# Keeping attention output channel-major from the value product to the output product, with the gate on GpSimd

## The chip, the cores and the metric

The kernel is a single program on one core of a Trainium2 chip. The metric is the device time of one execution in microseconds (us); of several runs the median is taken. The engines that matter are TensorE (PE, with its weight loads as PEld), VectorE (DVE), ScalarE (ACT), GpSimd (POOL) and SyncE (SP), which here only issues DMAs.

## The reference, cut to what matters

One transformer block over 2048 rows of 512 channels in float32: adaptive layer norm, attention of 32 heads of 16 channels, computed in 4 segments of 512 rows, with a compressive memory between segments, then a feed-forward layer with 1792 hidden units. The attention part is:

```
for s in range(4):                       # segments of 512 rows
    logits = einsum("bhqd,bhkd->bhqk", qs, ks) * scale + mask
    p = softmax(logits, axis=-1)
    a_dot = einsum("bhqk,bhkd->bhqd", p, vs)
    pq = phi(qs)                         # phi(t) = t + 1 if t > 0 else exp(t)
    num = einsum("bhld,bhde->bhle", pq, M)
    den = einsum("bhld,bhd->bhl", pq, z)[..., None] + 1e-6
    a_mem = num / den
    o = g * a_mem + (1.0 - g) * a_dot    # g = sigmoid(beta), one number per head
    M = M + einsum("bhld,bhle->bhde", pk, vs)
    z = z + einsum("bhld->bhd", pk)
x = x + ga * (concat(o) @ wo)            # then a second layer norm and
x = x + gb * (relu(h @ w1 + b1)**2 @ w2 + b2)
```

In segment 0 the memory is empty, so `o` there is only `(1 - g) * a_dot`.

## The kernel before

**Units.** Attention is worked in 16 units `u = 4*s + cc`: segment `s` and a group `cc` of 128 channels, which are 8 heads. A unit has two quads (`qd` 0 and 1) of 4 heads. The dense products are done in two float32r parts (high and low) with three matmuls for each product: high·high, high·low, low·high.

**What a unit runs.** `qk` makes q and k with the channels on partitions (`bqk`, L734); ACT and DVE copy them to `sg`, and SP's DMAs put each head's 16 rows at its place in `ST`. `a_quad` computes scores (`ba`, L847) only to find each row's maximum, which DVE takes (L852); the maxima are turned on PE (`bat`, L917), copied by ACT to `mt`, and written by DMA into a spare row of `ST`. `b_quad` computes the scores again with the maximum subtracted by that row (`bpb`, L1017), ACT takes the exponential (L1034), POOL cuts the causal triangle (L1021), and `bpv` (L1076) multiplies by the values. Its result has channels on partitions: one bank of 128 partitions by 512 rows for a quad, 32 partitions per head, of which the first 16 are the head's output channels and the 17th is the softmax denominator. ACT copies the bank to `oraw` (L1100).

**The way back to rows.** After both quads, `turn_o` (L1107) transposes the unit's output by 16 small matmuls (`bfin`, L1111) in two phases, between which a one-element POOL memset (`hinge`, L493) keeps apart two row tiles that swap banks. The normalisation (`norms`: reciprocal L1138, product with 1-g L1140, product L1141) is then done by DVE with rows on partitions, into `on`.

**The memory.** `mem` reads the memory with 16 small matmuls per unit of segments 1 to 3 (`bmr`, L944), also with rows on partitions, and DVE gates it (`den` L951, reciprocal, `am` L954). POOL adds `am` to `on` (L1147), SP stores `on` to `o_dram` in DRAM (L1150). In the last segment the add is on DVE, and the result stays on the chip in `X1L`. The rest of `mem` (`pkt`, `bmu`) updates the memory block `MB`.

**The output product.** `wo_tile(g)` takes 128 rows: it loads `ot` from `o_dram` (L1198) and the block's input rows `xw` (L1199), turns `ot` by 4 transposes (`bwot`, L1209), splits it into high (ACT, L1215) and low (DVE, L1217) parts `oT`, does 12 matmuls (`bwop`, L1182 to L1184), adds the input (DVE, L1224) and takes the statistics of the second layer norm. `blnq` (L599) are that norm's transposes, after which DVE and ACT apply scale and shift (`ln_affine`, L605 and L607) and split the result into the feed-forward's input `H2a` (L612). The feed-forward is `bh` (L1342 to L1344) and `bpf` (L1370 to L1372), with weights loaded through two buffers `wr` (L1308, L1316).

**The order.** The program is a list of nodes with an engine, a cost, a due time, predecessors, and buffers taken from pools of fixed size. The order on each engine is not the planner's choice: the table `ORDER` holds the node numbers of every engine in sequence, and the engine's next node is always the next number. `pe("R")`, `pe("C")` and `pe("F")` mark work that uses the PE array as 64-row tiles, as 32-column tiles, or whole. The first feed-forward node waits for all the nodes of attention:

```
N_FFN = op("NIL", 0.0, open_ffn, -20.0, after=list(PL.nodes))
```

Of the kernel before, what the change touches and what calls it, by code (L numbers as in the profile page):

```python
# [18 lines left out]
P = 128  # L19
# [39 lines left out]
8 47 28 68 41 32 70 49 56 17 35 3 23 66 27 83 58 85 92 16 40 75 65 87 89 14 22 94 15 19 10 96 98 106 112 59 43 63 42  # L59
124 29 55 62 25 45 67 60 73 50 61 118 74 34 24 9 46 48 172 162-163 173 164 174 77 175 51 36 165 31 52 166 69 167 37  # L60
168 64 176 20 53 169 177-178 30 72 26 179 11 39 13 57 12 18 76 21 38 71 44 54 33 327-330 198 332 199 333-334 200-201
232 335 242 203-205 240 206 484-485 251 486-487 245 270 489-490 237 491 215-218 492 261 220-221 247 222 356 264 223
259 747 742 273 608-609 256 275 610 427 282 611 290 285 613 278 614 364 615 266 616 366 375 369 294 383 752 295-296
430 298 385 361 305 308 757 551 371 313 380 301 554 513 388 398 317 518 432 390 318-319 532 761 321 439 762 323 435
763 447 764 521 526 406 451 442 766 455 767 675 523 768-769 458 542 414 452-453 537 528 400 408 416 462 470 866 637
422 928 540 465 929-930 645 545 474-476 424 556 931 650 563 933-934 642 935 547 559 936 794-795 656 647 796-797 478
566 799-800 480 571 801-802 661 575 652 579 576 582 999 586 678 577 589 669 828 598 594 666 1061 664 680 599-600 687
671 1062 836 1063 690 602 1064 847 604 683 1066-1067 695 841 1068 869 1069 838 833 1342 699-701 703 811 855 812 710
# [141 lines left out]
2369 2368 2371-2372 2276 2375 2379 2570 2377-2378 2540 2376 2295 2580 2550 2398 2590 2560 2417 2600 2638 2746 2645  # L210
2637 2736 2636 2766 2673 2756 2641 2652 2659 2680 2648 2666 2687 2676 2694 2655 2776 2662 2701 2669 2697 2729 2715
2683 2708 2690 2722 2704 2718 2711 2732 2725 3569 3153 3156 3364 3358 3563 2948 3361 2951 3566 3159 3367 2954 3572
2957 3162
""",
}

# [1205 lines left out]
```

## Time and profile before

| | before |
|---|---|
| median of 3 runs | 811.79 us (811.22 to 814.17) |
| profiled execution, its own time | 813.31 us |
| its span, first to last instruction | 811.6 us |
| mean granted PE clock | 0.975 |
| PE busy | 790.8 us, 97% of the span, 6177 instructions |
| PE weight loads busy | 617.7 us, 76% |
| DVE busy | 539.8 us, 67% |
| ACT busy | 441.8 us, 54% |
| POOL busy | 222.3 us, 27% |
| DMA traffic | 65.35 MB, mean 81 GB/s |

How to read it: the span is what the profiler saw from the first instruction to the last; the execution's own time has 1.7 us around it. Busy shares are over the whole span, and the span has stages of two kinds: attention until about 472 us, and the feed-forward after it. The profile's rows that the prediction uses are shown there.

### The profile page before, as it was taken

Reading aid. Unit: us, or ns where it says so; the run is one execution under the profiler, and the core shown is the slowest. Engines: PE = TensorE matmul, PEld = TensorE weight load, DVE = VectorE, ACT = ScalarE, POOL = GpSimd, SP = SyncE. Lnnn points to the kernel's source line nnn. Section 1 sums busy time; section 2 is a strip of 40 time slices with the busy share of each in tenths; the row PEclk is TensorE's granted clock in tenths of the full one; section 3 lists DMA queues with packets and bytes.
Section 4 is the critical chain, followed back from the end, with each engine's and each line's share of the span. In section 5 each row is a group of like instructions: output and inputs, shape, how many; then the busy total and the mean of one; then the engine's idle time right before and its main releaser. Section 6 shows DMA issues by size and latency. Waiting matters only on the chain.

```text
span 811.6 us, 16841 instructions
## 1 busy us (share of the span) xinstructions
PE 790.8 (97%) x6177; PEld 617.7 (76%) x6177; DVE 539.8 (67%) x1514; ACT 441.8 (54%) x950; POOL 222.3 (27%) x334
## 2 busy tenths in 40 slices
PE   9999999999998999999999989999999999999997
PEld 8988667686776757876667658888887888888886
DVE  5478859888778797879988877786545343223223
ACT  1457976879876798588855744544223323222221
POOL 3263464347555476354522210000000000000000
PEclk7899989999999999999999999999999999999999
DMA  9454572234133251334532133321100010001001
GB/s 319 123 137 126 163 200 80 71 92 96 52 93 93 63 127 54 99 76 109 154 101 80 53 117 95 101 78 53 40 13 1 1 39 14 1 1 52 1 1 52
DMA packets 51308, 65.35 MB, mean 81 GB/s; under 512 B 7829, under 2 KB 24985, under 8 KB 51226
## 3 DMA queue, kind: packets, MB, share of 16 engines
q1 hardware_dynamic: 51074, 64.14, 28.2%
q8 instruction: 49, 0.80, 0.4%
q14 instruction: 33, 0.27, 0.1%
q10 hardware_dynamic: 152, 0.13, 0.0%
HBM read 29.91 MB, written 7.34 MB: 46 GB/s over the span
## 4 chain that ended last, share of the span: by engine, by line
PE 55%; DVE 5%; ACT 1%; issue 1%; POOL 0%; DVEq 0%; ACTq 0%
PE bh L1342 6%; PE bh L1343 6%; PE bh L1344 6%; PE bpf L1370 6%; PE bpf L1371 6%; PE bpf L1372 6%; PE bqk L734 3%; PE bpv L1076 3%; PE bpb L1017 2%; PE ba L847 2%; PE bwop L1182 2%; DVE ba L852 1%; PE bv L814 1%; PE bwop L1183 1%; PE bwop L1184 1%; PE bwot L1209 1%
## 5 line engine op out<-in xcount | busy, mean ns | idle before, releaser
L852 DVE CUSTOM_DVE_ANT_0 ba<-ba,msk 128x512 f32<-128x512 f32 (+2 forms) x384 | 185.9, 542 | 44.8 <-PE ba L847 39.2
L1034 ACT ACTIVATE pt<-bpb 128x512 f32<-128x512 f32 x320 | 173.3, 609 | 27.0 <-PE bpb L1017 25.3
L1359 DVE TENSOR_TENSOR r<-r 128x512 f32<-128x512 f32 x56 | 38.7, 691 | 128.1 <-ACT rr L1356 128.1
L1021 POOL TENSOR_SCALAR_AFFINE_SELECT pt<-pt 128x512 f32<-128x512 f32 x128 | 80.1, 644 | 89.6 <-ACT pt L1034 71.2
L734 PE MATMUL bqk<-HT,WQK 64*128 64x512 f32 x720 | 104.2, 398 | 0.0
L1352 ACT ACTIVATE r<-bh,b1c 128x512 f32<-128x512 f32 x56 | 38.5, 688 | 108.4 <-DVE rr L1360 55.8
L1370 PE MATMUL bpf<-W,rr 128*128 128x512 f32 x224 | 88.2, 394 | 0.0
L1371 PE MATMUL bpf<-W,rr 128*128 128x512 f32 x224 | 87.6, 391 | 0.0
L1372 PE MATMUL bpf<-W,rr 128*128 128x512 f32 x224 | 87.5, 391 | 0.0
L1017 PE MATMUL bpb<-ST 64*128 64x256 f32 (+2 forms) x512 | 82.8, 361 | 2.4 <-DVE oT L1217 0.5
L1076 PE MATMUL bpv<-pt,VT 128*32 128x512 f32 (+3 forms) x1024 | 81.8, 445 | 0.6 <-POOL pt L1021 0.3
L847 PE MATMUL ba<-ST 63*128 63x256 f32 (+2 forms) x512 | 78.1, 347 | 2.5 <-DVE mx L852 2.1
L734 PEld LDWEIGHTS bqk<-HT,WQK 64*128 64x128 f32 x720 | 74.2, 186 | 6.4 <-ACT ac L885 1.7
L1017 PEld LDWEIGHTS bpb<-ST 64*128 64x128 f32 x512 | 52.9, 188 | 24.8 <-DVE mx L852 5.9
L847 PEld LDWEIGHTS ba<-ST 63*128 63x128 f32 x512 | 54.8, 189 | 20.9 <-DVE mx L852 4.7
L1356 ACT ACTIVATE rr<-r 128x512 fp32r<-128x512 f32 x56 | 35.4, 632 | 55.9 <-PE bpf L1372 55.2
L605 ACT ACTIVATE lnf<-blnq,modc 128x128 f32<-128x128 f32 x88 | 34.2, 470 | 43.0 <-PE blnq L599 40.8
L1076 PEld LDWEIGHTS bpv<-pt,VT 128*32 128x32 f32 x1024 | 27.6, 111 | 36.0 <-issue 27.5
L814 PE MATMUL bv<-WVO,HT 64*128 64x512 f32 x384 | 54.2, 395 | 0.8 <-ACT phi L780 0.8
L852 DVE DVE_READ_ACCUMULATOR2_ANT mx<- 128x1 f32 x384 | 53.7, 140 | 0.0
L1372 PEld LDWEIGHTS bpf<-W,rr 128*128 128x128 f32 x224 | 42.1, 188 | 9.1
L1370 PEld LDWEIGHTS bpf<-W,rr 128*128 128x128 f32 x224 | 42.1, 188 | 9.1
(164 smaller groups left out, 1528.8 us busy)
## 6 DMA issues: line engine op xcount, KB each, us to landing
ST<-sg SPq DMA_DIRECT2D x192, 128.0 KB
wr<-in_B_w SPq DMA_DIRECT2D x28, 256.0 KB
xt<-in_A_x SPq DMA_DIRECT2D x16, 256.0 KB
wm<-in_w_mod SPq DMA_DIRECT2D x16, 256.0 KB
xw<-in_A_x SPq DMA_DIRECT2D x16, 256.0 KB
o_dram<-on SPq DMA_DIRECT2D x12, 256.0 KB
ot<-o_dram SPq DMA_DIRECT2D x12, 256.0 KB
out<-X SPq DMA_DIRECT2D x12, 256.0 KB
```

The source lines that it names most:

```text
L734: m = nc.tensor.matmul(bank(("qk", u, w)), W3(w, k, x, cc * P, (cc + 1) * P)[z], HT[z, y, k], start=(ph == 0 and k == 0 and i == 0), stop= ...
L814: m = nc.tensor.matmul(bank(("v", s, t)), HT[z, x, k, t * P:(t + 1) * P], WVO[z, k, y], start=(ph == 0 and k == 0 and i == 0), stop=(ph == ...
L847: nc.tensor.matmul(dst[:, c0:c0 + n], ST[b:b + 63, 0, sl, qt * P:(qt + 1) * P], ST[b:b + 63, 1, sl, :n], start=True, stop=True)
L852: nc.vector.tensor_tensor_reduce(i, i, msk[:, 512 - n:], scale=1.0, scalar=-3e38, op0=ALU.add, op1=ALU.max, accum_out=o)
L1017: nc.tensor.matmul(dst, ST[b:b + 64, 1, sl, kb * P:(kb + 1) * P], ST[b:b + 64, 0, sl, q0:512], start=True, stop=True)
L1021: nc.gpsimd.affine_select(out=ap, in_=ap, pattern=[[0, ap.shape[1]], [1, P]], compare_op=ALU.is_ge, fill=0.0, base=0, channel_multiplier=-1)
L1034: ns = [act(512, lambda j=j: nc.scalar.activation(buf("PPP"[n], pt)[:, i + j], bank(keys[j]), AF.Exp, scale=0.25), pr[slot] + 0.01 + 0.001 ...
L1076: nc.tensor.matmul(bank(o)[32 * hq:32 * hq + 32, q0:q0 + src.shape[1]], v[:, a:a + 32], src, start=start, stop=stop, tile_position=(0, 32 ...
L1342: nc.tensor.matmul(p, wh, h2[:, 0, k], start=(k == 0), stop=False)
L1370: nc.tensor.matmul(p, rh, FF["W2"][:, f, 0], start=(f == 0), stop=False)
L1371: nc.tensor.matmul(p, rh, FF["W2"][:, f, 1], start=False, stop=False)
L1372: nc.tensor.matmul(p, rl, FF["W2"][:, f, 0], start=False, stop=(f == NF - 1))
```

## The change

The output of the value product is not turned back to rows. It goes to DRAM as it is and comes back with the unit's 128 channels packed on 128 partitions; it is gated there, and the output product takes its stationary operand from it directly.

- `turn_o`, its hinge and `norms` go, and so do the 4 transposes `bwot` of every `wo_tile`, the pools `am` and `on`, and `o_dram`.
- The memory is read with channels on partitions too: two matmuls of 68x512 (`bmr`, now L950) in the place of 16 of 128x68; ACT copies both to `ar` (L954) and SP stores `ar` to `o_raw` (L956). `ar` shares the pool of two buffers with `oraw`, which now holds both quads.
- A new function `heads_out` follows each unit: SP stores `oraw` to `o_raw` (L1119, 512 KB), loads the denominators `den` (L1132, L1134) as 128 partitions of 32 numbers, and the packed values into slots 0 and 2 of `X1L` (L1137, L1140). DVE makes the factors g/den and (1-g)/den on 128x2x32 numbers (L1145 to L1149), SP stores them to `o_gate` (L1153) and loads each back, repeated for the 16 channels of a head, into slots 1 and 3 of `X1L` (L1156). POOL does two products and one sum of 128x512 (L1159; in segment 0 one product), and SP stores the result to `o_turned` (L1174). The 4 slots of `X1L` are one set, used by one unit after another.
- `wo_tile` loads `ot` from `o_turned` with channels on partitions (L1220); ACT makes the high part (L1235), and the low part is on POOL (L1237), in the last segment on DVE. `xw` is a load of its own (L1224).
- The last segment's gating nodes (`LATE`) are no longer ahead of `N_FFN`, so the feed-forward's first nodes may stand before them.
- The gate's numbers `ge` and `omg` are one per partition and group (4 small loads in place of one), a pool `lnf` of two buffers takes over a use of `oraw`, and the `ORDER` tables of all engines are new. The planner's constants are the same.

```diff
-            def read():
-                for t in range(4):
-                    for r in (0, 1):
-                        z = slice(64 * r, 64 * r + 64)
-                        nc.tensor.matmul(bank(bs[r])[:, t * 4 * VA:(t + 1) * 4 * VA], TL[q_][z, t * P:(t + 1) * P],
-                                         MB[z, cc, r * 4 * VA:(r + 1) * 4 * VA], start=True, stop=True)
+            def read():
+                for r in (0, 1):
+                    z = slice(64 * r, 64 * r + 64)
+                    nc.tensor.matmul(bank(bs[r])[:4 * VA, :], MB[z, cc, r * 4 * VA:(r + 1) * 4 * VA], TL[q_][z, :], start=True, stop=True)
...
+            n = [act(512, lambda r=r: nc.scalar.copy(buf("oraw", ar)[:4 * VA, r], bank(bs[r])[:4 * VA, :]), pr[0] + 0.01, after=[n], put=[bs[r]])
+                 for r in (0, 1)]
+            AMN[u] = sp(lambda: nc.sync.dma_start(o_raw[u][2 * P:].rearrange("(r p) n -> p r n", r=2), TL[ar][:4 * VA]), pr[0] + 0.02, 1 << 18,
+                        after=n, put=[ar])
...
+    def heads_out(u, pr):
...
+        def load_d():
+            nc.sync.dma_start(den()[:, 0], rows(0, 2 * P, 32)[:, DH].rearrange("h (i j) -> h i j", j=32))
+            if s:
+                nc.sync.dma_start(den()[:, 1], rows(2 * P, VROW, VA)[:, DH].rearrange("h (i j) -> h i j", j=32))
...
+        def store_g():
+            m = 2 if s else 1
+            nc.sync.dma_start(o_gate[u][0:m].rearrange("o h (i j) -> (h i) o j", j=32), den()[:, 0:m])
+        def load_g(i):
+            nc.sync.dma_start(X1L[:, 1 + 2 * i], o_gate[u][i][:, None, :].to_broadcast([NB, DH, 512]))
+        def times(k, f, op_):
+            return lambda: nc.gpsimd.tensor_tensor(X1L[:, k], X1L[:, k], X1L[:, f], op=op_)
...
+        if s:
+            lg.append(in_turn(3, sp(lambda: load_g(1), pr + 0.06, 1 << 18, after=[w], **own(3))))
+            m.append(op("POOL", 1.24, times(2, 3, ALU.mult), pr + 0.07, after=[lg[1], l[2]], **done(3)))
+            m.append(op("POOL", 1.24, times(0, 2, ALU.add), pr + 0.08, after=m, **done(2)))
+        OUT[u] = sp(lambda: nc.sync.dma_start(o_turned[s][cc * P:(cc + 1) * P, :], X1L[:, 0]), pr + 0.09, 1 << 18, after=[m[-1]], **done(0))
+        if s == NS - 1:
+            LATE.extend(l + [g, w] + lg + m + [OUT[u]])
...
-        n = pe("F", 0.387, tr, pr, after=heads + [N_FFN] if last else [ld], get=[("#D", b), (pool, ot)], put=() if last else [o])
...
-        l = dve(512, lambda: nc.vector.tensor_tensor(TL[ot][:, 1], bank(b), TL[ot][:, 0].bitcast(F32), op=ALU.subtract), pr + 0.01,
-                after=[h], put=[b])
+        l = op("DVE" if last else "POOL", 0.6 if last else 1.24, lambda: (nc.vector if last else nc.gpsimd).tensor_tensor(
+            TL[ot][:, 1], TL[o], TL[ot][:, 0].bitcast(F32), op=ALU.subtract), pr + 0.01, after=[h], put=[o])
...
-    N_FFN = op("NIL", 0.0, open_ffn, -20.0, after=list(PL.nodes))
+    N_FFN = op("NIL", 0.0, open_ffn, -20.0, after=[n for n in PL.nodes if n not in LATE])
```

Three places of the new order. First SP's queue between two units, before, in segment 2: `on` is an attention output going to DRAM, `mt` and `sg` are the rows for `ST`.

```order
L925 DMA ST<-mt 1x8x128 x2
L1150 DMA o_dram<-on 128x4x128
L925 DMA ST<-mt 1x8x128 x2
L789 DMA ST<-sg 32x2x512 x12
L925 DMA ST<-mt 1x8x128 x2
```

The same queue after, around the gating of unit 9 (segment 2): `o_raw_74` is the packed output, `o_raw_75` the memory's part of the same unit, `o_gate_90` the factors.

```order
L1140 DMA X1L<-o_raw_74 128x1x512
L1119 DMA o_raw_74<-oraw 128x2x512
L935 DMA ST<-mt 1x8x128 x2
L1132 DMA den<-o_raw_74 128x1x32
L1137 DMA X1L<-o_raw_74 128x1x512
L1134 DMA den<-o_raw_75 128x1x32
L1153 DMA o_gate_90<-den 128x2x32
L1156 DMA X1L<-o_gate_90 128x1x512 x2
L935 DMA ST<-mt 1x8x128 x2
```

Where one store stood between the rows for `ST`, there are now seven issues that wait on one another, with `mt` rows between and behind them.

Second, POOL in the same segment, before: `pt` are the triangles of the exponentials, `ac` of the row maxima.

```order
L1021 AFFINE_SELECT pt<-pt 128x4x128 x4
L1147 TENSOR_TENSOR on<-on,am 128x512
L893 AFFINE_SELECT ac<-ac 128x4x128
L493 MEMSET hinge_s 1x1
L1021 AFFINE_SELECT pt<-pt 128x4x128
```

POOL after, at unit 9's gating (`hinge_s` here is a hinge of the value projection `bv`, which PE waits for):

```order
L1018 AFFINE_SELECT pt<-pt 128x4x128
L903 AFFINE_SELECT ac<-ac 128x4x128
L1159 TENSOR_TENSOR X1L<-X1L 128x512
L497 MEMSET hinge_s 1x1
L1159 TENSOR_TENSOR X1L<-X1L 128x512 x2
L1018 AFFINE_SELECT pt<-pt 128x4x128 x4
```

A hinge and four triangles now stand behind products that wait for the loads of `o_gate`.

Third, PE at the end of attention, before: the last value products, then the way to the first feed-forward products.

```order
L1076 MATMUL bpv<-pt,VT_113 32x256 x4
L599 MATMUL blnq<-ident,xh 128x128 x4
L1111 MATMUL bfin<-ident,oraw 128x64 x16
L1209 MATMUL bwot<-ident,X1L 128x128 x12
L1182 MATMUL bwop<-WVO,oT 128x512
```

PE after, behind the last value products:

```order
L1073 MATMUL bpv<-pt,VT_148 32x512 x4
L1073 MATMUL bpv<-pt,VT_148 32x384 x4
L1073 MATMUL bpv<-pt,VT_148 32x128 x4
L1073 MATMUL bpv<-pt,VT_148 32x256 x4
L1205 MATMUL bwop<-WVO,oT 128x512
```

and, 47 further `bwop` and 8 further `blnq` later, the first feed-forward products:

```order
L1207 MATMUL bwop<-WVO,oT 128x512
L609 MATMUL blnq<-ident,xh 128x128 x8
L1362 MATMUL bh<-H2a,W_7341 128x512
L1363 MATMUL bh<-H2a,W_7341 128x512
L1364 MATMUL bh<-H2a,W_7341 128x512
```

Four output tiles (48 `bwop`) and all 16 norm transposes of the feed-forward's first input now stand between the last value products and the first `bh`; before, most of them stood ahead of the last value products.

DVE at the same place, before: the last normalisation, the low parts of two output tiles, and the low parts of the first three weight tiles `W_7749`, which `bh` multiplies with.

```order
L1141 TENSOR_TENSOR X1L<-bfin,dn 128x4x64
L1138 RECIPROCAL dn<-bfin 128x16
L1140 TENSOR_TENSOR dn<-dn,omg 128x16
L1141 TENSOR_TENSOR X1L<-bfin,dn 128x4x64
L1147 TENSOR_TENSOR X1L<-X1L,am 128x4x128
L1217 TENSOR_TENSOR oT<-bwot,oT 128x512 x2
L1311 TENSOR_TENSOR W_7749<-wr,W_7749 128x512 x3
```

DVE after: `X_6173` are the rows of segment 2, `X_6171` those of segment 0, which `xh`, `lnf` and `H2a` take to the first feed-forward product.

```order
L605 TENSOR_SCALAR xh<-X_6171,st_all 128x512
L1244 TENSOR_TENSOR X_6173<-bwop,xw 128x512
L589 BN_STATS bs<-X_6173 128x6
L590 BN_AGGR st_all<-bs 128x2
L605 TENSOR_SCALAR xh<-X_6171,st_all 128x512
L617 TENSOR_SCALAR lnf<-blnq,modc 128x128 x2
L1244 TENSOR_TENSOR X_6173<-bwop,xw 128x512
L605 TENSOR_SCALAR xh<-X_6171,st_all 128x512
L589 BN_STATS bs<-X_6173 128x6
L590 BN_AGGR st_all<-bs 128x2
L617 TENSOR_SCALAR lnf<-blnq,modc 128x128 x4
L622 TENSOR_TENSOR H2a<-lnf,H2a 128x4x128 x3
```

The adds and statistics of segment 2 stand between the steps that make the first feed-forward input, and the weights' low parts behind them.

More of the change, by code (lines that the diff above doesn't have):

```diff
@@ L64 @@
[L64 to L68, printed above, removed]
@@ L209 @@
[L209 to L213 removed]
+88 78 91 80 84 82 93 97 79 81 129 86 95 140 130 161 150 139 149 159 740 742-743 741 186-187 191 189 188 190 197 194
@@ L372, in block_kernel @@
     dram = ctx.enter_context(tc.tile_pool(name="dram", bufs=1, space=bass.MemoryType.DRAM))
-    o_dram = dram.tile([S, D], F32, name="o_dram")
+    o_turned = [dram.tile([D, L], F32, name=f"o_turned{s}") for s in range(NS)]
+    o_raw = [dram.tile([2 * P + VROW, 512], F32, name=f"o_raw{u}") for u in range(NU)]
+    o_gate = [dram.tile([2, NB, 512], F32, name=f"o_gate{u}") for u in range(NU)]
     wpool_s = ExitStack()
@@ L470, in block_kernel @@
     PL.held["pad"] = [("pk", PL.pools["pk"].pop(0))]
-    ge = small.tile([P, H], F32, name="ge", bufs=1)
+    ge = small.tile([P, 4], F32, name="ge", bufs=1)
     def silu():
@@ L533, in mod_parts @@
         t = ("t", "mod", m)
-        MODT[m] = act(512, lambda: nc.scalar.copy(buf("oraw", t), bank(b)), pr + 0.03, after=[n], get=[("oraw", t)], put=[b])
+        MODT[m] = act(512, lambda: nc.scalar.copy(buf("lnf", t), bank(b)), pr + 0.03, after=[n], get=[("lnf", t)], put=[b])
         return t
@@ L1098, in b_quad @@
         VUSE[u].append(k)
-        r, b, on = ("oraw", u, qd), ("fin", u, qd), ("on", u)
-        ORW[u, qd] = act(512, lambda: nc.scalar.copy(buf("oraw", r), bank(o)), p_fin, after=[k, ORW.get((u - 1, 1))], get=[("oraw", r)], put=[o])
-        if qd == 0:
-            return
-        last = s == NS - 1
-        tail = []
-        def turn_o(ph):
-            for t in range(4):
-                for r in (0, 1):
-                    z = slice(64 * r, 64 * r + 64)
-                    m = nc.tensor.transpose(bank(("fin", u, ph ^ r))[:, t * P + 64 * r:t * P + 64 * r + 64],
-                                            TL["oraw", u, ph ^ r][z, t * P:(t + 1) * P], ident[z, z])
-                    if ph == 0 and t == 3:
-                        tail.append(m)
-                    if ph and t == 0:
-                        swap(m, tail)
@@ L1192, in wo_tile, with load_x @@
         last = s == NS - 1
[L1193 removed]
+        o, xk, b2, ot = ("ot", g), ("xw", g), ("wop", g), ("oT", g)
         pool = "rr" if last else "oT"
         def load():
[L1197 to L1198 removed]
+            nc.sync.dma_start(buf("xr", o).rearrange("p (k n) -> p k n", k=KD),
+                              o_turned[s][:, (g % 4) * P:(g % 4 + 1) * P].rearrange("(k p) n -> p k n", p=P))
+        def load_x():
             nc.sync.dma_start(buf("xr", xk), xs[g * P:(g + 1) * P, :])
         heads = [OUT[u] for u in range(4 * s, 4 * s + 4)]
[L1201 to L1202 removed]
+        free = [N_FFN if last else N_LATE]
+        ld = sp(load, pr - 0.2, 1 << 18, after=heads + free, get=[("xr", o)])
+        lx = sp(load_x, pr - 0.15, 1 << 18, after=free, get=[("xr", xk)])
         if last:
[L1204 to L1210 removed]
+            XWN.append(lx)
         def hi():
```

409 lines of the change are left out of this document (204 added, 205 removed), and 7 rows, old and new, of the table ORDER.

## The prediction

> **What bounds the kernel now.** I read the page's first parts, then the waits of PE, then busy time by stage, then the rows of the steps that go. The page (part 1, and part 4, which follows the work that ended last back to the start):
>
> ```profile
> span 811.6 us, 16841 instructions
> PE 790.8 (97%) x6177; PEld 617.7 (76%) x6177; DVE 539.8 (67%) x1514; ACT 441.8 (54%) x950; POOL 222.3 (27%) x334
> PE 55%; DVE 5%; ACT 1%; issue 1%; POOL 0%; DVEq 0%; ACTq 0%
> ```
>
> PE is busy for 97% of the span, and the chain is PE. The longest wait of PE (total, times, longest), then three stages (busy us of PE, PEld, DVE, ACT, POOL with counts; PE clock, DMA share, GB/s) and the end of attention:
>
> ```profile
> PE bwot L1209 <- DVE X1L L1147: 3.7, 1, 3.7
> ...
> 178.00:227.00 49.00, 46.98 (x574) 33.54 (x573) 40.94 (x142) 42.61 (x98) 30.32 (x49) 0.97 0.25 62
> 276.00:325.00 49.00, 47.17 (x585) 32.83 (x583) 39.58 (x134) 42.95 (x97) 33.69 (x48) 1.00 0.38 97
> 423.00:472.00 49.00, 48.26 (x393) 32.97 (x391) 43.35 (x123) 30.56 (x65) 13.19 (x21) 1.00 0.19 61
> 475.00:481.00 6.00, 2.65 (x11) 2.56 (x12) 4.45 (x13) 1.86 (x4) 0.00 (x0) 0.77 0.70 212
> ```
>
> PE hardly waits, except once, where attention ends. So a microsecond taken from PE in a stage is a microsecond of time, as long as the next engine allows it: ACT holds 42.95 of 49 us in one stage and 42.61 in another, DVE 43.35 at the end of attention.
>
> **What goes from PE.** PE's records of the steps that go, in order of time (start, duration; starts are what count, since ends overlap):
>
> ```profile
> 319.92 0.46 PE L1017 MATMUL bpb<-ST 64*128 64x256 f32 x4
> 320.16 1.61 PE L734 MATMUL bqk<-HT,WQK 64*128 64x512 f32 x12
> ...
> 325.49 0.41 PE L1111 MATMUL bfin<-ident,oraw 64*128 64x64 f32 x8
> 325.71 0.94 PE L734 MATMUL bqk<-HT,WQK 64*128 64x512 f32 x6
> 457.72 0.46 PE L1111 MATMUL bfin<-ident,oraw 64*128 64x64 f32 x8
> 458.44 0.90 PE L1017 MATMUL bpb<-ST 64*128 64x512 f32 x4 [0.26 <-DVE X L1224]
> ...
> 462.20 0.48 PE L1017 MATMUL bpb<-ST 64*128 64x256 f32 x4
> 462.62 0.66 PE L1209 MATMUL bwot<-ident,ot 128*128 128x128 f32 x4
> 463.03 0.48 PE L1182 MATMUL bwop<-WVO,oT 128*128 128x512 f32 x1
> ```
>
> - *The way back (`bfin`).* 16 units of two phases. A phase costs 0.22 us at 325.49 and 0.72 at 457.72 (with the switches around it). 32 phases give 7.0 to 23.0; I take 0.44, a little nearer the cheap one since only a few of these phases wait: 14.1.
> - *Transposes of `wo_tile` (`bwot`).* Four take 0.41 (462.62 to 463.03): 12 tiles are 4.9. The last segment's are in the tail:
>
> ```profile
> 472.10 0.66 PE L599 MATMUL blnq<-ident,xh 128*128 128x128 f32 x4
> ...
> 474.11 0.55 PE L1209 MATMUL bwot<-ident,X1L 128*128 128x128 f32 x3
> 478.35 2.18 PE L1209 MATMUL bwot<-ident,X1L 128*128 128x128 f32 x9 [3.69 <-DVE X1L L1147]
> 480.18 0.78 PE L1182 MATMUL bwop<-WVO,oT 128*128 128x512 f32 x1
> 480.75 0.63 PE L1183 MATMUL bwop<-WVO,oT 128*128 128x512 f32 x1
> 481.18 0.59 PE L1184 MATMUL bwop<-WVO,oT 128*128 128x512 f32 x1
> 481.61 0.39 PE L1182 MATMUL bwop<-WVO,oT 128*128 128x512 f32 x1
> 481.84 0.40 PE L1183 MATMUL bwop<-WVO,oT 128*128 128x512 f32 x1
> ```
>
>   Three are 0.55, the wait 3.69, nine more 1.83 (to 480.18), the last four 0.41: 6.5, and 11.4 in all. The first three `bwop` behind the wait take 0.57, 0.43 and 0.43 where later ones take 0.23: 0.7 of low clock that goes too.
> - *Reading the memory (`bmr`).* Sixteen small matmuls cost 0.92 (313.40 to 314.32). For the new form, two 512-row matmuls on two row tiles, the nearest row is the value product: eight records on four column tiles, two records to a float32 matmul, cost 0.88 (300.67 to 301.55).
>
> ```profile
> 300.67 1.07 PE L1076 MATMUL bpv<-pt,VT 128*32 128x512 f32 x8
> 301.55 0.48 PE L978 MATMUL bmu<-VT,pk 128*32 128x34 f32 x32
> ...
> 313.40 1.15 PE L944 MATMUL bmr<-MB,phi 64*128 64x68 f32 x16
> 314.32 1.00 PE L734 MATMUL bqk<-HT,WQK 64*128 64x512 f32 x6
> ```
>
>   Twelve units: a gain of 0.5. Were the two tiles to run one after the other, it would be 1.76, a loss of 10; I take 0.5, since the small ones already run on two row tiles.
> - *Switches.* The transposes were full-array work between row-tile work. The new order has 22 fewer changes between whole array and row tiles and 4 more between column and row tiles. One costs 0.42 (462.20 to 462.62) less 0.24 (319.92 to 320.16, the same work without a change): 0.18. 18 by 0.18 are 3.2.
>
> Together 14.1 + 11.4 + 0.7 + 0.5 + 3.2 = 29.9 us.
>
> **What comes in.** DVE loses the gates and norms and gains one small gate per unit; ACT gains two copies a unit in segments 1 to 3, POOL two more operations of 128x512 there (three where one add was) and 12 low parts `oT`, SP about ten issues a unit. Prices, by groups (total, mean ns | idle before):
>
> ```profile
> L1147 POOL TENSOR_TENSOR on<-on,am 128x512 f32<-128x512 f32 x8 | 10.3, 1285 | 1.0 <-DVE on L1141 1.0
> L1138 DVE RECIPROCAL dn<-bfin 128x16 f32<-128x16 f32 x32 | 8.0, 249 | 5.1 <-PE bfin L1111 5.1
> L1100 ACT COPY oraw<-bpv 128x512 f32<-128x512 f32 x32 | 18.9, 590 | 18.0 <-PE bpv L1076 12.6 <-PE bmodr L1266 4.3 <-POOL HT L612 0.6
> L607 DVE TENSOR_SCALAR lnf<-blnq,modc 128x128 f32<-128x128 f32 x40 | 14.3, 403 | 15.1 <-ACT lnf L605 15.1
> L612 DVE TENSOR_TENSOR H2a<-lnf,H2a 128x512 fp32r<-128x512 f32 x8 | 5.5, 684 | 0.5 <-ACT H2a L612 0.5
> L1224 DVE TENSOR_TENSOR X<-bwop,xw x12: 672/682/692, 397.7 to 469.7; 128x512 f32<-128x512 f32 x12
> L579 DVE BATCH_NORM_STATS2 bs<-X x12: 661/683/697, 413.3 to 474.4; 128x6 f32<-128x512 f32 x12
> L595 DVE TENSOR_SCALAR xh<-X,st_all x12: 517/540/856, 453.9 to 585.8; 128x512 f32<-128x512 f32 x12
> L1173 DVE TENSOR_TENSOR wo<-wo,gab x4: 684/960/1120, 379.7 to 391.2; 128x512 f32<-128x512 f32 x4
> 481.65 0.37 SPq L1308 DMA_DIRECT2D wr<-in_B_w  x1
> 484.52 0.62 ACT L1310 CAST W<-wr 128x512 fp32r<-128x512 f32 x1 [2.14 <-DMA wr<-in_B_w]
> ```
>
> - *ACT.* Two units start in a 49 us stage: 4 by 0.59 is 2.4 more, 45.4 us. The stage with 42.95 shrinks by some 2 us to 47 and would then be 97% ACT. With its like in the segment before (42.61) I charge 2.5 for both (0 if the copies fall into ACT's gaps, 5 if all of them show).
> - *The tail.* Behind the last value products PE now has 48 `bwop` and 16 `blnq` ahead of the first `bh`: 48 by 0.23 and 16 by 0.10 are 12.7. The first `bh` waits for DVE, whose list from the second of the four output tiles on is 3 adds (0.68), 3 statistics (0.68, with an estimated 0.18 to aggregate, less than the small reciprocal's 0.25), 8 affine steps (0.40), 4 `H2a` (0.68), 3 `xh` (0.54), a gate (0.75, an estimate: three small operations by the reciprocal's 0.25) and a weight's low part (0.68, as `H2a`): 13.6. It starts when 24 `bwop` and four `blnq` are through, some 6.9. So `bh` comes at 20.5 and PE idles 7.8 (0 if ACT's share and a different overlap of adds and waits shorten the list, 13.6 if none is covered). Before, most of this list ran beside value products.
> - *Weights there.* W1's third tile waits for one of two `wr` buffers to come back: a 256 KB load lands in 2.87 (481.65 to 484.52), with cast and low part about 4.5 against 2.8 of `bh` work (12 by 0.23): 1.7 (0 to 5).
> - *Clock.* Two waits this long, each followed by 0.7 as above: 1.5.
> - *DVE beside POOL.* `wo` (L1173) takes 684 ns alone and up to 1120 beside POOL's work. Two such in the tail's list, each longer by up to 0.44: 0.9 (0 to 3.9, three POOL operations of 1.29). The Trainium skill, "SBUF — State Buffer", section "Who interferes with whom", says that a DVE operation with two inputs in SBUF and a GpSimd operation that reads SBUF cannot run at once: the second is held for the whole of the first. The stretched row agrees in direction, though not in size; by the rule the result would be up to 3 us later.
> - *The last segment's way.* Copy, store, load, gate, store, load, three products, store, load, cast and low part are five transfers by 2.9, three POOL operations and 3 us of small ones, 21.4 at the least. `bh` of the first tiles covers what lies behind 20.5, so nothing is charged (0 to 6).
> - *SP and DMA.* Ten issues of some 0.6 us lengthen no chain of PE while the DMA share is 0.38; the rows for `ST` are written well ahead. Nothing (0 to 5).
>
> Costs: 2.5 + 7.8 + 1.7 + 1.5 + 0.9 = 14.4. The span goes from 811.6 to 811.6 - 29.9 + 14.4 = 796.1, the profiled execution from 813.31 to 797.8, and the median, which stands 1.5 below that execution, to 796.3.
>
> **Rivals.**
> 1. *POOL stops PE: slower.* POOL runs in order. A hinge that the next value projection needs, and triangles, stand behind products that wait for the factors' loads. That way is a copy (0.59), four transfers by 2.87, a gate (0.75) and a product (1.29): 14.1. PE has 96 matmuls of `bqk` and `bv` (0.134 each, 1.61 by 12), 50 score matmuls (0.06, 0.24 by 4) and 16 value products (0.11, 0.88 by 8) before it needs the hinge: 17.7. While transfers take 2.9 there is no stall. At 3.8 a transfer the cover is gone; at 4.4 twelve units lose 2.5 each, 30, and the time is 826. It ends above 816 from 4.2 on. For it: DMA share 0.38 with seven issues behind others in one queue; against: the slack of 3.6.
> 2. *ACT is the bound in segments 1 to 3.* Then the gain there is mostly lost: 24 copies by 0.59 are 14.2 in all, of which 10 more would show: 806. For it: the row 42.95 of 49; against: 30.56 in the last stage.
> 3. *A shorter tail and a faster DVE.* If the list of DVE is covered as before, 7.8 and 1.7 go, and 787 results; with `bfin` at 0.6 a phase, 782.
> 4. *The whole tail shows* (13.6 idle, port 3.9, loads 5): 808, no change that counts.
>
> **How the numbers follow.** About 0.5%, 4 us, is what a measurement of this kernel can tell from no change, so the same is 807.7 to 815.9. The likeliest, all steps as priced within their middle bounds, 788 to 804: 0.57. Rival 3, 781 to 788: 0.12. Rival 2, up to 807.7: 0.13. Rival 4, or part of rival 1: 0.10. Rival 1 in full: 0.08. Faster 0.82, same 0.10, slower 0.08. The range leaves out the outer ends of both sides: 783 to 809, and the likeliest one's own is 788 to 804.
>
> **What would show it.** Right: PE busy down by about 20 us, no `bfin` and `bwot`; `bmr` at 0.9 us a unit; a wait of `bh` for DVE (`H2a` or W1) of 6 to 10 us where attention ends; PE waits of below 5 us in segments 1 to 3. Wrong: PE waiting for a hinge or a triangle on POOL by more than 1 us in each unit (rival 1); ACT above 95% in segment 1 or 2 with PE waiting for `pt` or `sg` (rival 2); `bmr` at 1.8; a tail in which the last segment's `bwop` wait for `oT`.

## The result, and the profile after

The changed kernel takes 886.25 us (median; 883.72 to 889.06) against 811.5 for the kernel before on the same chip (809.3 to 814.17): 1.092 times as long, with a 95% interval of 1.087 to 1.097. That is 74.8 us more, where 15.5 less were predicted.

The page of the kernel after: span, busy time with instruction counts, DMA traffic, and the shares of the chain that ended last.

```profile
span 883.2 us, 16094 instructions
PE 793.8 (90%) x5713; PEld 600.2 (68%) x5713; DVE 501.8 (57%) x1374; ACT 453.0 (51%) x974; POOL 277.1 (31%) x362
DMA packets 75688, 94.70 MB, mean 107 GB/s; under 512 B 16757, under 2 KB 35961, under 8 KB 75610
PE 38%; DMA 7%; DVE 2%; ACT 1%; SPq 1%; issue 0%; POOL 0%; DVEq 0%; ACTq 0%
```

The PE instructions are gone as meant (6177 to 5713), yet PE's busy time did not fall (790.8 before), and its idle time went from 20.8 to 89.4 us. No other engine is near full: ACT is at 51%. DMA is now 7% of the chain, where before it had no entry, and moves 94.70 MB (65.35 before). So something waits, and the next view says for what. PE's waits after (total, times, longest):

```profile
PE bpb L1014 <- DMA ST<-mt: 29.2, 8, 8.5
PE bh L1362 <- ACT W L1330: 10.1, 2, 9.3
PE bqk L744 <- POOL hinge_s L497: 8.2, 1, 8.2
PE blnq L609 <- DVE xh L605: 5.0, 2, 4.0
PE bv L824 <- DVE mx L862: 4.8, 1, 4.8
```

The largest item names neither the gating nor the output product but the row of maxima `mt`, whose DMA the change does not touch. It is issued by SP, so SP's own waits are read next:

```profile
...
SPq L1132 <- DMA o_raw<-oraw: 49.4, 12, 7.2
...
SPq L1174 <- POOL X1L L1159: 24.4, 6, 8.1
SPq L1156 <- DMA o_gate<-den: 24.0, 12, 5.8
...
SPq L1153 <- DVE den L1149: 11.6, 9, 2.3
...
SPq L1137 <- DMA o_turned<-X1L: 9.3, 4, 4.4
```

The lines left out are waits for DVE and ACT: those of the feed-forward's weight loads and output stores, of the `mt` rows, and of the store of `oraw` for its copies. Every line shown is a step of `heads_out` that stands at the head of SP's queue until an earlier transfer has landed or DVE or POOL has finished, and everything behind it in that queue stands too. One such place, in time: SP (start, duration of issue), then PE.

```profile
194.07 0.40 SPq L1119 DMA_DIRECT2D o_raw<-oraw  x1
201.72 0.64 SPq L1132 DMA_DIRECT2D den<-o_raw  x1
202.41 0.62 SPq L1137 DMA_DIRECT2D X1L<-o_raw  x1
203.09 0.58 SPq L1134 DMA_DIRECT2D den<-o_raw  x1
203.76 1.37 SPq L935 DMA_DIRECT2D ST<-mt  x2
207.04 0.95 PE L1014 MATMUL bpb<-ST 64*128 64x512 f32 x2 [8.50 <-DMA ST<-mt]
```

The 512 KB store is issued at 194.07. The load of the denominators, which reads what it writes, leaves at 201.72, 7.65 us later. The `mt` rows stand behind that load, leave at 203.76, and PE has been idle for 8.50 us when they land. The Trainium skill, "DMA: Bandwidth & Descriptors", section "Anatomy of one DMA — SWDGE (gpsimd) path", says that DMA engines do not wait on semaphores: the wait is held by the issuing sequencer before dispatch; the gap from 194.07 to 201.72 in SP's own queue agrees. The fit on the same page of the Trainium skill, 2.0 us plus bytes at 436 GB/s, made for another issue path, would give an estimated 3.2 us here; the trace has 7.65, behind some dozen other transfers.

The stages show where the loss lies (first from the start to the last value product, then to the first `bh`, then to the end of PE's work; busy us of PE, PEld, DVE, ACT, POOL; PE clock, DMA share, GB/s). Before:

```profile
0.00:472.20 472.20, 460.45 (x4702) 347.60 (x4703) 378.69 (x1216) 333.04 (x766) 222.16 (x333) 0.96 0.40 110
472.20:482.30 10.10, 6.10 (x38) 4.94 (x39) 7.39 (x17) 4.83 (x10) 0.09 (x1) 0.83 0.61 182
482.30:806.90 324.60, 324.23 (x1439) 265.15 (x1437) 152.50 (x280) 103.91 (x176) 0.00 (x0) 1.00 0.10 32
```

After:

```profile
0.00:514.60 514.60, 445.48 (x4210) 320.46 (x4210) 326.73 (x1044) 338.64 (x779) 266.51 (x354) 0.92 0.51 147
514.60:545.30 30.70, 16.34 (x69) 12.72 (x65) 17.18 (x47) 7.92 (x16) 8.81 (x7) 0.76 0.60 172
545.30:878.70 333.40, 331.94 (x1440) 267.01 (x1440) 156.52 (x283) 106.49 (x179) 1.74 (x1) 0.99 0.12 38
```

Attention is 42.4 us longer, the stretch to the first `bh` 20.6, the feed-forward 8.8.

### The profile page after: what moved, and what is told of

The parts are those of the page before. It is cut to its first block, busy times and chain, and to the rows that moved or that the text cites. A ratio compares the mean times of both kernels' runs of the same rounds, so it can differ in the third digit from the quotient of the medians.

```text
span 883.2 us, 16094 instructions
## 1 busy us (share of the span) xinstructions
PE 793.8 (90%) x5713; PEld 600.2 (68%) x5713; DVE 501.8 (57%) x1374; ACT 453.0 (51%) x974; POOL 277.1 (31%) x362
## 2 busy tenths in 40 slices
DMA packets 75688, 94.70 MB, mean 107 GB/s; under 512 B 16757, under 2 KB 35961, under 8 KB 75610
## 5 line engine op out<-in xcount | busy, mean ns | idle before, releaser
L862 DVE CUSTOM_DVE_ANT_0 ba<-ba,msk 128x128 f32<-128x128 f32 (+2 forms) x384 | 186.2, 542 | 113.2 <-PE ba L857 104.2
L1014 PE MATMUL bpb<-ST 64*128 64x256 f32 (+2 forms) x512 | 85.0, 371 | 34.3 <-DMA ST<-mt 29.2
L1073 PE MATMUL bpv<-pt,VT 128*32 128x512 f32 (+3 forms) x1024 | 90.7, 479 | 6.9 <-DVE X L1244 3.1
L1014 PEld LDWEIGHTS bpb<-ST 64*128 64x128 f32 x512 | 56.2, 198 | 57.8 <-issue 32.5
L857 PE MATMUL ba<-ST 63*128 63x256 f32 (+2 forms) x512 | 82.8, 369 | 4.6 <-DVE mx L862 1.8
L1159 POOL TENSOR_TENSOR X1L<-X1L 128x512 f32<-128x512 f32 x40 | 51.7, 1296 | 39.6 <-DMA X1L<-o_gate 29.7
L1073 PEld LDWEIGHTS bpv<-pt,VT 128*32 128x32 f32 x1024 | 29.8, 118 | 45.1 <-issue 33.8
L1362 PE MATMUL bh<-H2a,W 128*128 128x512 f32 x112 | 45.8, 409 | 10.1 <-ACT W L1330 10.1
L1390 PEld LDWEIGHTS bpf<-W,rr 128*128 128x128 f32 x224 | 42.1, 188 | 9.7
```

Of the source, the lines that this page charges most:

```text
L857: nc.tensor.matmul(dst[:, c0:c0 + n], ST[b:b + 63, 0, sl, qt * P:(qt + 1) * P], ST[b:b + 63, 1, sl, :n], start=True, stop=True)
L862: nc.vector.tensor_tensor_reduce(i, i, msk[:, 512 - n:], scale=1.0, scalar=-3e38, op0=ALU.add, op1=ALU.max, accum_out=o)
L1014: nc.tensor.matmul(dst, ST[b:b + 64, 1, sl, kb * P:(kb + 1) * P], ST[b:b + 64, 0, sl, q0:512], start=True, stop=True)
L1073: nc.tensor.matmul(bank(o)[32 * hq:32 * hq + 32, q0:q0 + src.shape[1]], v[:, a:a + 32], src, start=start, stop=stop, tile_position=(0, 32 ...
L1362: nc.tensor.matmul(p, wh, h2[:, 0, k], start=(k == 0), stop=False)
L1390: nc.tensor.matmul(p, rh, FF["W2"][:, f, 0], start=(f == 0), stop=False)
```

## The experiments

The theory: SP's in-order queue is blocked by the chain's waits, and the rows for `ST` and the loads behind it come late. The rivals: POOL's products and the hinge behind them (rival 1 of the prediction); the transfers themselves, by issue slots and bytes; the new order, whatever the transfers. One thing matters for reading these runs: the table does not hold SP's queue. The kernel's manual order covers PE, DVE, ACT and POOL; SP's order is set by the scheduler, which put the load of `den` close behind the store that it waits for. In the trace the load stands directly behind that store in 8 of the 16 units; in 4 of them `mt` rows stand between the two, as in the unit that is listed ahead of the prediction. Ratios are to the kernel before in the same comparison (medians 810.4 to 812.3), with 95% intervals.

**The same kernel without the chain** (`no_chain`): `oraw`'s first half is stored straight to `o_turned`; no loads, gate, or products.

```diff
+        def none(*_):
+            pass
+        load_d = load_o = load_a = gate = store_g = load_g = none
+        times = lambda *_: none
```

> The changed kernel without the gating: the denominators, the packed values and the factors are not loaded, DVE's gate and POOL's products are left out, and the 128x512 of the first quad's copy goes to o_turned as it is. PE's work and the orders of PE, ACT and DVE stay. If the chain of transfers is what costs the time (theories Q and B), this is the gain that was forecast for PE with a shorter tail: 780 to 800 us. Theory O (the orders of PE, ACT and DVE wait for each other in a new way): above 840.

802.9 us (801.5 to 805.8), ratio 0.9896 [0.9869, 0.9923], just above the 780 to 800 that were expected. Page and stages:

```profile
PE 770.5 (96%) x5713; PEld 590.7 (74%) x5713; DVE 481.5 (60%) x1330; ACT 451.5 (56%) x974; POOL 226.3 (28%) x322
0.00:446.40 446.40, 425.60 (x4210) 312.31 (x4211) 309.74 (x1006) 337.59 (x779) 223.72 (x320) 0.96 0.49 142
446.40:463.60 17.20, 13.35 (x64) 10.49 (x64) 14.40 (x40) 7.82 (x17) 2.59 (x2) 0.99 0.46 148
463.60:795.30 331.70, 331.50 (x1440) 267.87 (x1440) 155.99 (x284) 106.12 (x179) 0.00 (x0) 0.99 0.12 37
```

The whole loss is the chain: without it, the rest of the change is 8.6 us faster than before, and the chain costs 83.4 (886.25 less 802.9). The spans differ by 83.2: PE idles 89.4 us instead of 29.5 (800.0 less 770.5), and the same 5713 instructions take 23.3 us more, at a mean granted clock of 0.939 instead of 0.973. And the `mt` rows, with the store's landing not awaited in the queue:

```profile
179.42 0.39 SPq L1120 DMA_DIRECT2D o_raw<-oraw  x1
181.79 2.10 SPq L935 DMA_DIRECT2D ST<-mt  x2
```

They leave 2.37 us after the same store's issue; in the changed kernel it was 9.69.

**The chain added to the kernel before** (`before_hops`): twelve units of dummy transfers that wait on one another, put behind the store of `on`.

```diff
+                for m in (0, 1):
+                    nc.sync.dma_start(den[:, m], here[m * P:(m + 1) * P, 0:32])
+                nc.sync.dma_start(hop_d[u].rearrange("o (p j) -> p o j", j=32), den)
```

> The kernel before, with transfers added behind each of its 12 stores of on, in the same place of SP's queue: two loads of 128x32 from what was just stored, a store of these 32 KB, and two repeated loads of 128x512 of it, into a part of the chip's memory that is free then. Nothing uses them. Theory Q: each unit holds SP's queue by two landings (5 to 12 us), beyond the 4 to 18 us that the rows of mt have in hand in some units: 825 to 875 us, with new waits of PE for ST<-mt. Theory B: 7 MB more, below 818. Theory O: 808 to 816.

823.5 us (823.0 to 826.5), ratio 1.0178 [1.0129, 1.0226]; attention ends at 485.7 instead of 472.2. SP waits there too:

```profile
SPq L1155 <- DMA o_dram<-on: 21.4, 12, 3.4
SPq L1158 <- DMA hop_d<-X1L: 13.9, 10, 3.6
```

Such a chain costs some 13 us even where nothing needs its result. Its store is of 256 KB and no POOL product lies in it; SP's waits for landings come to 35.3 us, half of the 73.4 after. The time is just below the expected 825 to 875, and the way was not the expected one: PE has no wait for `mt` in this trace. It idles 28.4 us instead of 20.8, and the same 6177 instructions take 5.6 more.

**The `mt` rows out of SP's queue** (`mt_act`, and `side_act` with `xw` and the first three weight tiles as well): ACT issues them.

```diff
-                nc.sync.dma_start(STf[64 * j + 63:64 * j + 64, 0, sl:sl + 2, :], TL[mt].bitcast(F32)[8 * j:8 * j + 8, :])
+                nc.scalar.dma_start(STf[64 * j + 63:64 * j + 64, 0, sl:sl + 2, :], TL[mt].bitcast(F32)[8 * j:8 * j + 8, :])
```

> The changed kernel, but the 64 transfers of the row maxima (ST<-mt) are issued by ACT, which makes mt, and not by SP. Theory Q: PE's waits for these rows, 29.2 us in 8 waits, fall below 6, and with the clock that these waits cost the time is 840 to 858 us; the waits for the weights at the end of attention (about 10 us) stay. Theory B: the rows land late all the same, above 875. Theory O: above 875.

> As the run with the row maxima on ACT, with the loads of the block's input rows (xw) and of the first three tiles of w1 issued by ACT too. Theory Q: the wait for the first weights (9.3 us) and DVE's waits for xw go, 10 to 25 us below the run with the maxima alone. Theory B and O: within 5 us of it.

875.5 us, ratio 1.0801 [1.0742, 1.0861], and 872.5, 1.0782 [1.0729, 1.0835]. From `mt_act`, PE's wait and then ACT:

```profile
PE bpb L1014 <- DMA ST<-mt: 8.8, 8, 2.4
...
222.68 2.83 ACTq L935 DMA_DIRECT2D ST<-mt  x2
225.56 0.58 ACT L895 COPY ac<-ba 128x512 f32<-128x512 f32 x1 [2.44 <-issue]
```

The wait for `mt` goes from 29.2 to 8.8, but only 11 us of time come back, where the theory had 28 or more, and `side_act` gives 3 more instead of 10 to 25. Part of the price is on ACT: each of the 64 issues holds it, for 0.63 us at the median, and the two above, among the longest pairs, for 2.83. All waits of PE for ACT together go from 17.0 to 33.1 us. So late `mt` rows are a part of the loss, and this remedy pays on the next engine.

**SP's queue held to the table** (`sp_manual`):

```diff
-    with tc.manual_schedule(engines={..., mybir.EngineType.Pool}):
+    with tc.manual_schedule(engines={..., mybir.EngineType.Pool, mybir.EngineType.SP}):
```

> The changed kernel with SP's order held to the table, too. In the changed kernel it is not: the load of den stands right behind the store that it waits for, with the table three or four transfers stand between. Theory Q: SP's waits for o_raw (49.4 us) fall by a third, since a landing of 5 to 7 us is longer than three issues of 0.65, and the time is 855 to 880. Theory B: no change, 880 to 890.

868.4 us (866.8 to 869.7), ratio 1.0697 [1.0678, 1.0716], as expected. SP's wait for `o_raw` falls from 49.4 to 17.5, PE's for `mt` from 29.2 to 3.2; a new one comes, and some 8 us are given back at the very end, where the output stores now stand last in SP's queue (the span ends 12.8 us behind the last PE instruction, in the changed kernel 4.5). So 56.6 us of the loss remain when the `mt` rows are hardly late any more.

```profile
PE bpv L1073 <- POOL pt L1018: 11.9, 9, 3.1
```

**Three that did not separate the theories.** `lag` lets each unit's loads read the unit before's data, `free_reads` lets them read the kernel's input, so that they wait for no store; `no_products` leaves POOL's products out.

> The changed kernel, but the loads of the denominators, of the packed values and of the factors read what the unit before has left in DRAM (units 0 and 4 read their own), so no load waits for a store just issued. Transfers, bytes, DVE and POOL work and all orders stay; the attention output is that of other units. Theory Q (SP's queue runs in order, and the loads that wait at its head for a store to land hold up the rows for ST and the weights behind them): SP's waits for o_raw and o_gate, 49.4 and 24.0 us, fall below 15 together, PE's waits fall from 89 to below 35 us, and the time is 800 to 825 us. Theory B (30 MB more traffic makes every transfer slow): still above 870. Theory O (the new orders of PE and POOL have lost cover): still above 860.

> The changed kernel with all its transfers, sizes, DVE and POOL work, but the loads of denominators, packed values and factors read the block's input in DRAM, so that none has to wait for a store; the attention output is meaningless. Theory Q (loads that wait at the head of SP's queue for the store before them): 800 to 830 us, PE's waits below 40 us. Theory B (the traffic of 30 MB more makes transfers land late): above 855. The run that read the unit before's data did not decide this, since its loads were moved up behind the stores that they then read (SP waited 37.9 us for o_raw there).

> The changed kernel without POOL's products and sums: all transfers of the gating and their waits stay, and o_turned gets the packed values ungated. It parts the two queues in which the gating can hold others up. If SP's queue does nearly all of it: 865 to 880 us, PE's waits for ST<-mt stay above 20. If POOL's queue (products that wait for their loads, with triangles and hinges behind them) does a good part: below 855, and the hinge's wait of 8.2 us goes.

876.8 (1.0843 [1.0785, 1.0901]), 860.6 (1.0605 [1.0553, 1.0656]) and 894.3 (1.1013 [1.0944, 1.1083]). In each the scheduler gave SP another queue: in `lag` the loads moved up behind the stores that they now read and waited 37.9 us there; in `free_reads` they waited for buffers instead (17.5 on POOL's `X1L`, 17.4 on the store `o_turned`); in `no_products` the load of the memory's part came to stand where it waited 49.0 us for the store that it reads, the store of the result waited 45.2 us for the load before it, and PE's wait for `mt` grew to 50.6. None takes one cost away alone, and the sign of the last says nothing on POOL. But all three came out above what the theory of SP's waits expected (800 to 825, 800 to 830, 865 to 880).

**The denominators by a way of their own** (`den_first`): 16 KB of them are stored ahead of the 512 KB, and loaded from there.

> The changed kernel with 16 KB of denominators stored ahead of each large store, and loaded from there, so that den waits for a small transfer and not for 512 KB. Theory Q: the landing that den waits for falls from 5 to 7.6 us to 2 to 3, but the load of the packed values still waits for the large store at the head of the queue, so that most of the wait moves there: 870 to 886. If it falls below 860, the size of the store was the cost and not the waiting as such.

888.9 us, 1.0949 [1.0891, 1.1007]: no gain. SP's wait at the load of `den` falls from 49.4 to 28.8 us, now for the small store, and the one for `o_gate` stays (24.5). The load of the packed values, which was expected to take over the rest, waits only 1.8 us for the big store, so why nothing is won stays open.

**POOL's products alone** (`products_only`): `no_chain` with the 40 products put back.

```diff
-        times = lambda *_: none
```

> The run without the gating, with POOL's 40 products and sums put back at their places (on what X1L holds, nothing is loaded). If the products as work on POOL, beside DVE, cost little: 803 to 812 us, as without them. If POOL's 52 us of work as such delays triangles or DVE: above 820.

809.6 us (806.4 to 813.3), ratio 0.9979 [0.9951, 1.0007]: 6.7 more than `no_chain` for some 51 us of POOL work (277.4 busy against 226.3). Stretched DVE work, which the prediction had, is there in the changed kernel: the same gate operation beside POOL's products, then alone.

```profile
490.74 0.79 DVE L1145 TENSOR_SCALAR den<-den,ge 128x32 f32<-128x32 f32 x1
529.48 0.23 DVE L1145 TENSOR_SCALAR den<-den,ge 128x32 f32<-128x32 f32 x1
```

**The chain put where it is ready** (`float2`, `float3`, `float6`): the planner adds 2, 3 or 6 us to each landing of the chain and takes its steps when they are due and ready, not by the table; SP's queue is held to the result. `float6` also lets the output stores go as they come due, and adds 3 us in the last segment. All other nodes keep their order; a rule of the planner that ties `qk` to the chain of an earlier unit is dropped.

```diff
+            q.xl = 6 if s < NS - 1 else 3
...
+            self.given[e] = [i for i in self.given[e] if not self.nodes[i].fl]
```

> The changed kernel with all its work and a correct gate, in another order on SP, POOL and DVE: the gating's transfers are planned with landings 3 us later than the plan assumes, each of them and each gate and product is put in its queue only when what it needs has landed by that plan, and SP's order is held too. The orders of everything else stay as in the table. Theory Q (the gating waits at the head of in-order queues, since its transfers land later than the orders assume): SP's waits for o_raw and o_gate fall below 20 us, PE waits less for ST<-mt and for POOL, 835 to 855 us. Theory B (the traffic makes all transfers late): above 870.

> As the run with 3 us, with landings 2 us later than the plan assumes. Theory Q: near it, 830 to 865; which is better tells what landing the order needs. Theory B: above 870.

> As the run with landings 3 us later, now 6 us in segments 0 to 2 and 3 us in the last, and the stores of the output issued as they come due (with 3 us they all stood at the end of SP's queue, 8 us beyond before's end). Correct gate. If waiting in the queues is what is left of the loss (theory Q), more distance between a transfer and what waits for it takes more of it away: 830 to 848 us. If traffic is what is left (theory B): 850 to 856, only the 8 us of the end are won.

861.5 (1.0618 [1.0560, 1.0677]), 865.2 (1.0649 [1.0583, 1.0714]) and 858.1 us (855.4 to 860.0; 1.0581 [1.0548, 1.0614]). The first two lose the same 8 us at the end as `sp_manual`. PE's longest waits in `float6`:

```profile
PE bh L1498 <- ACT W L1466: 12.2, 2, 10.0
PE bpb L1146 <- DMA ST<-mt: 6.2, 3, 2.9
PE bpv L1205 <- DVE den L1277: 5.9, 2, 4.5
```

All three missed what was expected of them (835 to 855, 830 to 865 and 830 to 848). The best of these orders takes back 28.1 us of the chain's 83.4: the waits shown are then for the last weights, for `mt` and for DVE's factors.

**What is left, taken apart in that order.** Five kernels on `float6`: loads that read the input (`float6_free`), no products (`float6_noprod`), no chain (`float6_none`), the same transfers with nothing waiting for them and no gate or products (`float6_traffic`), and these with 16 numbers per partition in the place of 480 (`float6_tiny`).

```diff
-            nc.sync.dma_start(X1L[:, 0, 0:480], xs[u * P:(u + 1) * P, 0:480])
+            nc.sync.dma_start(X1L[:, 0, 0:16], xs[u * P:(u + 1) * P, 0:16])
```

> The same order with the loads of the gating reading the block's input, so that no load waits for a store; sizes, places, gates and products are the same (the attention output is meaningless). It takes RAW waits away with no transfer moved. Theory Q: 815 to 830 us, nearer the 810 of the run with products and without transfers. Theory B: within 6 us of the run with the true loads.

> The same order as the 6 us run with true loads, without POOL's products and sums (o_turned gets ungated values). If what is left is POOL's queue (triangles behind products that wait for the factors, 25.6 us of such waits in the 3 us run): 15 us or more below the 6 us run. If SP's queue or traffic: within 6 us of it.

> The 6 us order without the gating (no loads of denominators, values or factors, no gate, no products, as in the first run without the gating; SP's order held). It is the floor of that order. 803 us if the order of the rest is as good as the scheduler's; above 825 if holding SP to the table is itself a part of what is left of the loss.

> The same, with all transfers of the gating put back at their places in SP's queue and in their sizes, but from and to data that nobody makes or uses: they wait for nothing and nothing waits for them. The difference to the run without them is the price of 8 issues a unit on SP and of their traffic, the difference to the true 6 us run (858) that of waiting. Theory Q: 5 to 12 us above the run without, 30 or more below 858. Theory B: within 12 us of 858.

> As the run with transfers that nobody waits for, but the loads of values and factors bring 16 numbers for each partition and not 480: the same issues at the same places, 0.8 MB a unit less. If the 17 us between it and the run without transfers are issue slots on SP (8 a unit by 0.6 us): 826 to 831 us. If they are traffic (later landings of the rows for ST): 814 to 820.

| | us | ratio, 95% | less than `float6` |
|---|---|---|---|
| `float6_free` | 850.1 | 1.0478 [1.0446, 1.0510] | 8.1 |
| `float6_noprod` | 850.0 | 1.0488 [1.0451, 1.0524] | 8.1 |
| `float6_traffic` | 830.5 | 1.0207 [1.0175, 1.0239] | 27.6 |
| `float6_tiny` | 823.7 | 1.0148 [1.0113, 1.0183] | 34.4 |
| `float6_none` | 813.7 | 1.0033 [1.0004, 1.0062] | 44.4 |

Transfers that nobody waits for cost 16.8 us: 10.0 for the issues and their packets (`tiny` less `none`; `tiny` has 76136 packets, as `traffic`, and `none` 60423) and 6.8 for the bytes. By the ratios it is 14, 9 and 5, each good to some 4 us. The other 27.6 are the chain as work that is waited for; awaited landings and products give 8 each when taken away alone, and the rest is left to DVE's gate, waits for buffers and the weights behind the chain, not told apart. All five results lie between the two ranges that were set for them: neither cause has the loss to itself. `float6_none` is 10.8 above `no_chain`, so this order, with SP held and the planner's rule dropped, has a price of its own: in it the chain costs 44.4 us instead of 83.4.

## Why the prediction was wrong

**The step that failed** is "SP and DMA. Ten issues of some 0.6 us lengthen no chain of PE while the DMA share is 0.38; the rows for `ST` are written well ahead. Nothing (0 to 5)." In its place stands the chain's 83.4 us. The DMA share of attention was 0.40 before and 0.51 after, and neither number shows what stands in SP's queue: most of the ten issues wait for an earlier landing or for a result, and what waits at the head holds up all behind it. The rows for `ST` were well ahead before (no wait of PE for `mt`), and after they are late in 8 places, 29.2 us. If issues, packets and bytes cost as much in the shipped order as in `float6`'s (16.8; not run in the shipped one), 66.6 us are left for waiting and for POOL's products (6.7 in `products_only`). Which waits these are is settled only in part: the kernels in which the `mt` rows are less late (8.8 and 3.2 us of waits) win back 11 to 18 us, 26 without the 8 at `sp_manual`'s end. The rest is spread over PE's waits for DVE, ACT and POOL, the weights and the lower clock, and how it divides stays open.

**The price of a hop** was 2.87 us, taken from one 256 KB load. The store of 512 KB behind other transfers let its reader go after 7.65 us, and those of `o_gate` held SP for up to 5.8. The DMA share does not tell the two apart: it is 0.48 around that load (481.6 to 484.6) and 0.44 around that store (193 to 202).

**Rival 1** (0.08, 826 us) had the right kind of mechanism and a point of decision, 4.2 us a transfer, that was passed. It named POOL's queue, and the larger direct wait of PE came by SP's: 29.2 us for `mt` against 8.2 for the hinge. POOL's share of the rest is not separated in the shipped order; in `float6`'s the products are worth 8.1 of 44.4. The rival's own wait came once in full:

```profile
287.80 1.96 SPq L1153 DMA_DIRECT2D o_gate<-den  x1
295.62 1.21 SPq L1156 DMA_DIRECT2D X1L<-o_gate  x2
299.54 1.26 POOL L1159 TENSOR_TENSOR X1L<-X1L 128x512 f32<-128x512 f32 x1 [9.65 <-DMA X1L<-o_gate]
300.74 0.09 POOL L497 MEMSET hinge_s<- 1x1 f32 x1
300.88 1.65 PE L744 MATMUL bqk<-HT,WQK 64*128 64x512 f32 x6 [8.17 <-POOL hinge_s L497]
```

POOL stands 9.65 us for the factors, the hinge behind the product comes late, and PE loses 8.17.

**What goes from PE** was right in sum, and partly by luck. From before to `no_chain`, PE's busy time falls by 20.3 (forecast: about 20), though `bmr` gave 5.0 more than forecast and the feed-forward took 7.3 of PE's time back. Attention gets 25.8 shorter, but some 12 of that is work that only moved: 47 of its 144 `bwop` and all 13 `blnq` of the second norm now stand behind the last value products (47 by 0.23, 13 by 0.10). The forecast for the stage is 14.1 + 4.9 + 0.5 + 3.2 for `bfin`, `bwot`, `bmr` and switches, less 2.5 for ACT, 20.2, and 12 for the move: 32, so the stage fell short by some 6. PE's idle time in it went from 11.8 to 20.8 us, where the 2.5 were charged. The gain of `bmr`, whose start to the next is 0.46 us and not the 0.88 carried over from the value product, is 12 by 0.42, the 5.0.

```profile
278.17 1.02 PE L950 MATMUL bmr<-phi,MB 64*68 64x512 f32 x4
278.63 0.86 PE L857 MATMUL ba<-ST 63*128 63x256 f32 x4
```

**The tail** had the place right and one wait missing. `no_chain` needs 17.2 us from the last value product to the first `bh` (forecast 20.5), the changed kernel 30.7, of which PE idles 14.4 (forecast 7.8 and 1.7):

```profile
524.48 1.09 PE L609 MATMUL blnq<-ident,xh 128*128 128x128 f32 x4 [4.00 <-DVE xh L605]
...
535.26 0.66 PE L609 MATMUL blnq<-ident,xh 128*128 128x128 f32 x4 [1.01 <-DVE xh L605]
...
535.45 0.60 SPq L1137 DMA_DIRECT2D X1L<-o_raw  x1
536.10 1.20 SPq L1156 DMA_DIRECT2D X1L<-o_gate  x2
537.34 1.01 SPq L1328 DMA_DIRECT2D wr<-in_B_w  x2
544.59 0.62 ACT L1330 CAST W<-wr 128x512 fp32r<-128x512 f32 x1 [6.36 <-DMA wr<-in_B_w]
545.26 0.80 PE L1362 MATMUL bh<-H2a,W 128*128 128x512 f32 x1 [9.34 <-ACT W L1330]
```

DVE's list, on which the forecast rested, makes 5.0 of it; the other 9.3 are the weights' load, which left SP only behind the loads of values and factors of the last unit. The weight load was costed by its landing and `wr` buffers, not by what stands ahead of it. The feed-forward is 7.1 longer already without the chain (331.7 against 324.6; forecast 1.7). Its first 6 us, `no_chain` and then before, in the columns of the stages:

```profile
463.60:469.60 6.00, 5.81 (x12) 3.72 (x12) 1.77 (x4) 1.17 (x3) 0.00 (x0) 0.50 0.75 219
482.30:488.30 6.00, 6.00 (x30) 4.91 (x28) 3.24 (x6) 1.32 (x3) 0.00 (x0) 1.00 0.44 131
```

At a granted clock of 0.50, behind a wait of 2.89 us for the weights, 12 products take the 6 us; at the 0.23 of the later ones they would take 2.8. That is 3.2 of the 7.1, and five more `bwop` in the stage are 1.2; the rest stays open.

**The other rivals.** ACT was no bound (51%). DVE beside POOL is real, 0.23 to 0.79 us for one operation, and with whatever else POOL's products disturb it costs 6.7 us in the whole kernel; the forecast had charged it in the tail alone (0.9, up to 3.9). The clock term, 1.5 for two long waits, was far short: from `no_chain` to the changed kernel busy PE time is 23.3 us more for the same instructions.

## What to carry to other kernels

Price a round trip through DRAM by what stands behind each of its waits in the in-order queues of SP, POOL and DVE, and not by the DMA share; where some urgent small transfer shares such a queue, look first whether it comes late. Take a landing time from a row of the same size behind the same traffic, and look at who sets the order of the DMA queue before trusting a listing of one unit. Here, moving the late issues to a compute engine moved part of their price there, and the best new order took back a third of the chain's cost, not the whole.

## What the runs showed of the hardware that was not expected

- Issuing a DMA costs ACT about as much as SP: 0.63 us at the median of 64 in `mt_act` (2.21 at the longest), where a pair took SP 1.37 (203.76 above).
- Reading the memory with two 512-column float32 matmuls on two 64-row tiles takes 0.46 us (278.17 above), half of what 16 matmuls of 68 columns took on the same tiles (0.92).
- Transfers that nobody waits for still cost 16.8 us in `float6`'s order, 10.0 of it with hardly any bytes.
- Beside 59.9 us more of idle time, PE needed 23.3 us more for the same instructions, at a mean granted clock of 0.939 against 0.973. The same in the held order: `float6` against `float6_none` idles 31.3 more and is busy 13.4 more. No run took waits and clock apart.
